# RWKV-5 attention followed by a smelu MLP on one core: blocks of 256 tokens in a written-out order, and one piece of smelu under a checked bound

## Chip, core and metric

The kernel runs on one core of a Trainium2 chip. The metric is the device time of one execution in microseconds (us). Five engines share the work: TensorE (PE, matrix products; PEld is its weight load), VectorE (DVE), ScalarE (ACT), GpSimd (POOL) and SyncE (SP), whose queue issues the DMAs here.

## What is computed

First an attention with a running state, for 4 batches, 8 heads, 768 tokens and 48 channels per head:

```
for t in range(S):
    cur = einsum('bhd,bhe->bhde', u[None] * kt, vt)
    y[:, :, t] = einsum('bhd,bhde->bhe', rt, state + cur)
    state = w[None, :, :, None] * state + einsum('bhd,bhe->bhde', kt, vt)
```

Its output is put together as x, 3072 tokens by 384 channels. Then an MLP with 2048 hidden channels:

```
h = x @ w_in
g = where(h >= 1, h, where(h <= -1, 0, (h + 1)**2 / 4))
out = g @ w_out
```

The function between the two products is smelu. For |h| <= 1 only its middle piece, (h+1)²/4, applies.

## The kernel before

**Attention.** The tokens of a batch are cut into 6 chunks of 128. A *unit* is one chunk c of one batch b; there are 24, ordered by chunk and then by batch. The generator `attention` (L151) makes one unit in five stretches that end at a `yield`.

1. *Preparation* (L156 to L168). K, R and V come in by three DMAs (`load`, L57, four units ahead). POOL writes K·Winv into `Kw` and R·Wpow into `Rw` (both padded to 64 channels a head, three buffers in turn), and K·u and then that times R into `KU`. ACT casts V to bf16, and DVE sums `KU` over each head into `diag`.
2. *Transposes* (L170 to L176). PE transposes the four head pairs of `Kw` and of `Rw` (8 instructions) into `tr`, and ACT copies it to `RK`.
3. *Scores* (L179 to L188). PE makes 8 products into two banks `AT_p`, and DVE multiplies each by the mask `umask` into `AT`.
4. *Output and state* (L190 to L228). PE adds up `st` (the state's increment) and `y`, POOL and DVE update the state `X` and its bf16 copy `Tbd`, POOL makes `VD` = V·diag, DVE adds x = VD + y.
5. *xT* (L230 to L233). PE transposes x in three pieces, and ACT copies them into the block's `xT`.

**MLP.** A block is one chunk of all four batches, so 512 tokens, and there are 6 blocks. `layer1(m, n)` (L240) makes 128 of the 2048 hidden channels: three matmuls with 512 columns into `h_p` (one PSUM bank), then smelu in three instructions: ACT clamps h (`cl`, L253), ACT squares it (`sq`, L254), DVE takes the larger of sq and h into `gT` (L255). `layer2(m, n)` (L259) makes four of the 16 matmuls with 384 columns that an output tile of 128 tokens takes; after the last, ACT copies `o_p` out (L273) and SP sends it to memory. The bf16 copies of the weights are made at first use, `w_in` on DVE (L245) and `w_out` on POOL (L265).

**Order.** The text (L291 to L303) first runs the four units of block 0, and then, for each block m and each n, layer1(m, n), layer2(m-1, n) and the next of the 20 attention stretches of block m+1. This is not the final order: the framework's scheduler orders each engine's queue by its own reckoning, so instructions of one engine may leave the order of the text. Within an engine the order is then fixed, and it waits on semaphores.

Of the kernel before, what the change touches and what calls it, by code (L numbers as in the profile page):

```python
# [16 lines left out]
def kernel(  # L17
# [11 lines left out]
    nc = tc.nc  # L29
# [10 lines left out]
    MT = B * C  # L40
# [14 lines left out]
    loaded = {}  # L55

    def load(i):  # L57
        b, c = units[i]
        t0 = c * C
        tiles = []  # L60
        for name, src in (("K", k), ("R", r), ("V", v)):
            t = io.tile([128, H, D], F32, name=name, tag=name)
            nc.sync.dma_start(out=t, in_=src[b, :, t0 : t0 + C, :].rearrange("h s d -> s h d"))
            tiles.append(t)
        loaded[i] = tiles
# [6 lines left out]
    u_bc = const.tile([128, H * D], F32, name="u_bc")  # L72
    nc.sync.dma_start(out=u_bc, in_=row_bcast(u))
    load(0)
# [9 lines left out]
    load(1)  # L84
# [3 lines left out]
    NQ = 4  # L88
    w_in_src = moe_w_in.rearrange("(ko ki) n -> ki ko n", ki=128)
    w_out_src = moe_w_out.rearrange("(no ni) d -> ni no d", ni=128)  # L90
    w_in_f, w_out_f = [], []
    for q in range(NQ):
        t = stage.tile([128, nKb, d_ff // NQ], F32, name=f"w_in_f{q}", tag="wf")
        nc.sync.dma_start(out=t, in_=w_in_src[:, :, q * (d_ff // NQ) : (q + 1) * (d_ff // NQ)])
        w_in_f.append(t)
        if q % 2 == 1:
            load(2 + q // 2)
    for q in range(NQ):
        t = stage.tile([128, nN // NQ, d_out], F32, name=f"w_out_f{q}", tag="wf")
        nc.sync.dma_start(out=t, in_=w_out_src[:, q * (nN // NQ) : (q + 1) * (nN // NQ), :])  # L100
        w_out_f.append(t)
# [9 lines left out]
    )  # L111
    i_int = const.tile([128, 1], mybir.dt.int32, name="i_int")
# [6 lines left out]
    nc.scalar.activation(lw, w_bc, AF.Ln)  # L119
    Wpow = const.tile([128, H, D], F32, name="Wpow")  # L120
# [3 lines left out]
    nc.scalar.activation(wc, wc, AF.Ln)  # L124
# [7 lines left out]
    NB = 3  # L132
    RWp, KWi = [], []
    for i in range(NB):
# [7 lines left out]
    for b in range(B):  # L142
# [3 lines left out]
        Tbd.append(t)  # L146


    xT = {}

    def attention(i):  # L151
        b, c = units[i]
        m = c
        if b == 0:
            xT[m] = gpool.tile([128, nKb, MT], BF16, name="xT", tag="xT")
        K, R, Vf = loaded.pop(i)  # L156
        if i + 4 < len(units):
            load(i + 4)
        Rw, Kw = RWp[i % NB], KWi[i % NB]
        nc.gpsimd.tensor_mul(Kw[:, :, 0:D], K, Winv)  # L160
        nc.gpsimd.tensor_mul(Rw[:, :, 0:D], R, Wpow)  # L161
# [3 lines left out]
        nc.gpsimd.tensor_mul(KU, K, u3)  # L165
        nc.gpsimd.tensor_mul(KU, KU, R)  # L166
        diag = work.tile([128, H], F32, name="diag", tag="diag")
        nc.vector.reduce_sum(diag, KU, axis=mybir.AxisListType.X)  # L168
        yield
        tr = ps_a.tile([128, 2 * NP, 128], BF16, name="tr", tag="a")  # L170
        for p in range(NP):
            nc.tensor.transpose(tr[:, NP + p, :], Kw[:, 2 * p : 2 * p + 2, :].rearrange("q h d -> q (h d)"), ident)  # L172
        for p in range(NP):
            nc.tensor.transpose(tr[:, p, :], Rw[:, 2 * p : 2 * p + 2, :].rearrange("q h d -> q (h d)"), ident)  # L174
        RK = work.tile([128, 2 * NP, 128], BF16, name="RK", tag="RK")
        nc.scalar.copy(RK, tr)  # L176
        RT, KT = RK[:, 0:NP, :], RK[:, NP : 2 * NP, :]
        yield
# [10 lines left out]
        yield  # L189
        if c < NCH - 1:  # L190
            st = ps_a.tile([128, NP, 2 * D], F32, name="st", tag="a")
            for p in range(NP):
                mm(
                    st[:, p, :], Kw[:, 2 * p : 2 * p + 2, :].rearrange("q h d -> q (h d)"),
                    V[:, 2 * p : 2 * p + 2, :].rearrange("q h d -> q (h d)"), start=True, stop=True,
                )
        y = ps_a.tile([128, H, D], F32, name="y", tag="a")
        first = True
        if c > 0:
            for p in range(NP):  # L200
                mm(  # L201
                    y[:, 2 * p : 2 * p + 2, :].rearrange("q h d -> q (h d)"), RT[:, p, :], Tbd[b][:, p, :],
                    start=first, stop=False, skip_group_check=True,
                )
                first = False
        for h in range(H):
# [4 lines left out]
            first = False  # L211
        if c < NCH - 1:
# [12 lines left out]
        VD = work.tile([128, H, D], F32, name="VD", tag="VD")  # L225
        nc.gpsimd.tensor_mul(VD, V, diag[:, :, None].to_broadcast([128, H, D]))  # L226
        x = work.tile([128, H * D], BF16, name="x", tag="x")
        nc.vector.tensor_add(x.rearrange("q (h d) -> q h d", h=H), VD, y)  # L228
        yield
# [3 lines left out]
        nc.scalar.copy(xT[m][:, :, b * C : (b + 1) * C], xp)  # L233
        yield


    gT = {}
    cast_in, cast_out = set(), set()

    def layer1(m, n):  # L240
        q = n // (nN // NQ)
        if q not in cast_in:
            cast_in.add(q)
            W = d_ff // NQ
            nc.vector.tensor_copy(w_in_sb[:, :, q * W : (q + 1) * W], w_in_f[q])  # L245
        if n == 0:
            gT[m] = gpool.tile([128, nN, MT], BF16, name="gT", tag="gT")
        h_p = ps_h.tile([128, MT], F32, name="h_p", tag="h")
        for kk in range(nKb):
            mm(h_p, w_in_sb[:, kk, n * 128 : (n + 1) * 128], xT[m][:, kk, :], start=(kk == 0), stop=(kk == nKb - 1))  # L250
        cl = ewp.tile([128, MT], F32, name="cl", tag="cl")
        sq = ewp.tile([128, MT], F32, name="sq", tag="sq")
        nc.scalar.activation(cl, h_p, IDENTITY_SAT240, scale=240.0)  # L253
        nc.scalar.activation(sq, cl, AF.Square, bias=0.5, scale=0.5 / 240.0)  # L254
        nc.vector.tensor_max(gT[m][:, n, :], sq, h_p)  # L255

    o_ps = {}

    def layer2(m, n):  # L259

        j, q = n // NQ, n % NQ
        if q not in cast_out:
            cast_out.add(q)
            W = nN // NQ
            nc.gpsimd.tensor_copy(w_out_sb[:, q * W : (q + 1) * W, :], w_out_f[q])  # L265
        if q == 0:
            o_ps[m, j] = ps_o.tile([128, d_out], F32, name="o_p", tag="o")
        o_p = o_ps[m, j]
        for f in range(q * (nN // NQ), (q + 1) * (nN // NQ)):
            mm(o_p, gT[m][:, f, j * C : (j + 1) * C], w_out_sb[:, f, :], start=(f == 0), stop=(f == nN - 1))  # L270
        if q == NQ - 1:
            o_sb = ewp.tile([128, d_out], F32, name="o_sb", tag="o_sb")
            nc.scalar.copy(o_sb, o_p)  # L273
            t0 = j * S + m * C
            nc.sync.dma_start(out=out[t0 : t0 + C, :], in_=o_sb)


    def attention_steps(m):
        for b in range(B):
            yield from attention(m * B + b)  # L280

    def drain(g, n):
        for _ in range(n):
            if next(g, "end") == "end":
# [49 lines left out]
```

## Time and profile before

| | us |
|---|---|
| median of 3 runs (lowest, highest) | 242.0 (240.9, 242.13) |
| the profiled execution | 240.13 |
| its span in the profile | 238.4 |
| busy: PE, ACT, POOL, DVE | 182.6, 164.3, 148.6, 137.2 |
| first matmul of the MLP starts at | 43.14 |

The profile is one execution. All rows below are on its time scale, which begins with the span. Busy times of PE overstate its work, since matmuls are pipelined and each one's row runs on into the next. The mean granted clock of TensorE was 0.97.

### The profile page before, as it was taken

How to read it: one execution, taken by the hardware profiler on the slowest of the kernel's cores; microseconds unless marked ns; L12 is line 12 of the kernel's file. 1: busy time of each engine (PE TensorE's matmuls, PEld its weight loads, DVE VectorE, ACT ScalarE, POOL GpSimd, SP SyncE). 2: the span in 40 equal slices, each digit the busy share in tenths (PEclk: the TensorE clock that was granted, in tenths of full speed). 3: DMA queues.
4: the chain of work that ended last, by engine and by line, in shares of the span. 5: the costliest groups of instructions: out<-in, count | busy, mean ns of one | idle time of the engine just before them, and what ended most of it. 6: DMA issues, size and time to landing. Idle time of an engine off the chain costs nothing.

```text
span 238.4 us, 4187 instructions
## 1 busy us (share of the span) xinstructions
PE 182.6 (77%) x1480; PEld 100.0 (42%) x1480; DVE 137.2 (58%) x245; ACT 164.3 (69%) x296; POOL 148.6 (62%) x197
## 2 busy tenths in 40 slices
PE   0033543796398296789797999899999999999994
PEld 0012322243255143445453545455555555445552
DVE  3008974167357426598656987688766666365400
ACT  3521312698469076969499897999979999699811
POOL 5297857979899998889999897955653000000000
PEclk9999999999859769999999999999999999999999
DMA  5999999945432048038775444400001001001121
GB/s 140 216 279 315 293 339 192 220 91 108 93 76 60 0 109 191 0 75 172 152 169 100 111 94 95 102 33 36 33 33 37 0 33 36 33 33 36 42 90 66
DMA packets 82772, 25.81 MB, mean 108 GB/s; under 512 B 75841, under 2 KB 81217, under 8 KB 82753
## 3 DMA queue, kind: packets, MB, share of 16 engines
q1 hardware_dynamic: 82752, 25.57, 43.9%
q8 instruction: 11, 0.18, 0.3%
q14 instruction: 9, 0.07, 0.1%
HBM read 20.84 MB, written 4.72 MB: 107 GB/s over the span
## 4 chain that ended last, share of the span: by engine, by line
PE 40%; POOL 22%; DVE 18%; issue 10%; ACT 7%; DMA 2%; SPq 0%; POOLq 0%; ACTq 0%; DVEq 0%
PE h_p L250 16%; PE o_p L270 16%; POOL KU L166 5%; POOL KU L165 4%; DVE gT L255 4%; POOL VD L226 3%; ACT sq L254 2%; ACT RK L176 2%; POOL KWi_158 L160 2%; POOL RWp_156 L161 2%; DVE x L228 2%; DMA K<-in_k_dram 2%; DVE diag L168 2%; ACT cl L253 2%; PE xp L232 2%
## 5 line engine op out<-in xcount | busy, mean ns | idle before, releaser
L250 PE MATMUL h_p<-xT,w_in_sb 128*128 128x512 bf16 x288 | 78.8, 391 | 9.7 <-DVE gT L255 9.1
L270 PE MATMUL o_p<-w_out_sb,gT 128*128 128x384 bf16 x384 | 80.8, 331 | 0.4 <-ACT o_sb L273 0.2
L255 DVE TENSOR_TENSOR gT<-sq,h_p 128x512 bf16<-128x512 f32 x96 | 64.0, 682 | 27.1 <-ACT sq L254 26.7
L253 ACT ACTIVATE cl<-h_p 128x512 f32<-128x512 f32 x96 | 56.2, 597 | 13.3 <-PE h_p L250 12.8
L254 ACT ACTIVATE sq<-cl 128x512 f32<-128x512 f32 x96 | 59.6, 635 | 1.6
L270 PEld LDWEIGHTS <-gT 128*128 128x128 bf16 x384 | 35.3, 98 | 25.2 <-issue 1.5
L168 DVE TENSOR_REDUCE diag<-KU 128x8 f32<-128x384 f32 x24 | 13.2, 551 | 50.8 <-POOL KU L166 40.1
L250 PEld LDWEIGHTS <-w_in_sb 128*128 128x128 bf16 x288 | 27.3, 100 | 34.4 <-issue 15.1
L233 ACT COPY xT<-xp 128x384 bf16<-128x384 bf16 x24 | 11.5, 477 | 26.2 <-PE xp L232 25.8
L176 ACT COPY RK<-tr 128x1024 bf16<-128x1024 bf16 x24 | 24.3, 1013 | 7.2 <-PE tr L174 7.2
L165 POOL TENSOR_TENSOR KU<-K,u_bc 128x384 f32<-128x384 f32 x24 | 24.0, 1001 | 2.2 <-DMA K<-in_k_dram 2.2
L226 POOL TENSOR_TENSOR VD<-V,diag 128x384 f32<-128x384 bf16 x24 | 19.9, 830 | 8.4 <-ACT V L163 6.6
L166 POOL TENSOR_TENSOR KU<-KU,R 128x384 f32<-128x384 f32 x24 | 24.0, 1002 | 0.4
L273 ACT COPY o_sb<-o_p 128x384 f32<-128x384 f32 x24 | 11.3, 474 | 14.2 <-PE o_p L270 14.1
L163 ACT CAST V<-V 128x384 bf16<-128x384 f32 x24 | 12.3, 513 | 5.7 <-DMA V<-in_v_dram 2.7
L228 DVE TENSOR_TENSOR x<-VD,y 128x384 bf16<-128x384 f32 x24 | 13.3, 553 | 1.0 <-PE y L207 0.4
L172 PE MATMUL tr<-ident,KWi_158 128*128 128x128 bf16 x32 | 3.8, 253 | 12.8 <-POOL KWi_158 L160 12.8
L160 POOL TENSOR_TENSOR KWi_158<-K,Winv 128x384 bf16<-128x384 f32 x8 | 8.0, 1001 | 8.7 <-ACT Winv L123 6.5
L232 PE MATMUL xp<-ident,x 128*128 128x128 bf16 x72 | 9.1, 243 | 4.8 <-DVE x L228 4.5
L183 PEld LDWEIGHTS <-RK 48*128 48x128 bf16 x192 | 5.9, 100 | 16.5 <-ACT RK L176 11.7
L201 PEld LDWEIGHTS <-RK 128*128 128x128 bf16 x80 | 5.5, 100 | 13.3 <-issue 10.8
L232 PEld LDWEIGHTS <-x 128*128 128x128 bf16 x72 | 5.1, 106 | 11.7 <-DVE x L228 10.9
(276 smaller groups left out, 248.0 us busy)
## 6 DMA issues: line engine op xcount, KB each, us to landing
K<-in_k_dram SPq DMA_DIRECT2D x24, 192.0 KB, 3.5
R<-in_r_dram SPq DMA_DIRECT2D x24, 192.0 KB, 3.5
V<-in_v_dram SPq DMA_DIRECT2D x24, 192.0 KB, 3.6
out_dram<-o_sb SPq DMA_DIRECT2D x24, 192.0 KB, 1.9
w_in_f_104<-in_moe_w_in_dram SPq DMA_DIRECT2D x1, 768.0 KB, 5.6
w_in_f_106<-in_moe_w_in_dram SPq DMA_DIRECT2D x1, 768.0 KB, 6.8
w_in_f_114<-in_moe_w_in_dram SPq DMA_DIRECT2D x1, 768.0 KB, 6.1
w_in_f_116<-in_moe_w_in_dram SPq DMA_DIRECT2D x1, 768.0 KB, 7.2
```

The lines of the kernel that those rows point to most:

```text
L165: nc.gpsimd.tensor_mul(KU, K, u3)
L166: nc.gpsimd.tensor_mul(KU, KU, R)
L168: nc.vector.reduce_sum(diag, KU, axis=mybir.AxisListType.X)
L176: nc.scalar.copy(RK, tr)
L226: nc.gpsimd.tensor_mul(VD, V, diag[:, :, None].to_broadcast([128, H, D]))
L228: nc.vector.tensor_add(x.rearrange("q (h d) -> q h d", h=H), VD, y)
L232: nc.tensor.transpose(xp[:, kk, :], x[:, kk * 128 : (kk + 1) * 128], ident)
L250: mm(h_p, w_in_sb[:, kk, n * 128 : (n + 1) * 128], xT[m][:, kk, :], start=(kk == 0), stop=(kk == nKb - 1))
L253: nc.scalar.activation(cl, h_p, IDENTITY_SAT240, scale=240.0)
L254: nc.scalar.activation(sq, cl, AF.Square, bias=0.5, scale=0.5 / 240.0)
L255: nc.vector.tensor_max(gT[m][:, n, :], sq, h_p)
L270: mm(o_p, gT[m][:, f, j * C : (j + 1) * C], w_out_sb[:, f, :], start=(f == 0), stop=(f == nN - 1))
```

## The change

The whole body from the pools down is rewritten in these respects.

- *Order.* Nearly everything is put in `tc.manual_schedule()`: each engine's queue follows the order of the text. The stretches of `attention` become five functions, `prep`, `s_tr`, `s_at`, `s_y` and `s_xp`, which the text calls in a written-out order.
- *Blocks.* A block is two units, 256 tokens; there are 12. `layer1(m, n)` makes two groups of 128 hidden channels, six matmuls with 256 columns into one PSUM bank. `layer2(m, n)` takes two hidden groups for both tiles of the block, four matmuls. All 12 `xT` are kept to the end.
- *smelu.* In the usual pass one ACT instruction, the square of (h+1)/2, goes from `h_p` to `gT`. Clamp, maximum and their buffers are gone there.
- *The bound.* |h| is at most |x||w| for the row x of a token and the column w of `w_in`. ACT sums x² for each token (`x2`, one more instruction a unit). POOL squares and adds up `w_in`, one quarter at a time, and PE and DVE finish the column sums (`w_norms`, 24 steps from step 48 of the main loop on). `bound_fails` compares the product of the two maxima with 0.95 and makes a flag. At the end all engines read the flag, and under `tc.If` a general pass (layer1 with clamp, square and maximum, and layer2) runs over all 12 blocks again.
- *Engines.* R·Wpow and K·u go from POOL to DVE. The casts of `w_in` are two pieces on DVE and one on ACT, those of `w_out` one on each. Half of the output copies go from ACT to DVE.
- *Buffers and loads.* Four instead of three `Rw`/`Kw`, six instead of five K, R, V, four PSUM banks for attention instead of three, two for `h_p` instead of three. At the start units 0 to 3 are loaded ahead of `w_in`, and the small loads for `wc` ahead of unit 0. The logarithm of `wc` goes ahead of the exponentials.

```
+    man = ExitStack()
+    man.enter_context(tc.manual_schedule())
...
+    def prep(i):
         K, R, Vf = loaded.pop(i)
+        Rw, Kw = RWp[i % NR], KWi[i % NR]
         nc.gpsimd.tensor_mul(Kw[:, :, 0:D], K, Winv)
-        nc.gpsimd.tensor_mul(Rw[:, :, 0:D], R, Wpow)
+        nc.vector.tensor_mul(Rw[:, :, 0:D], R, Wpow)
...
-        nc.gpsimd.tensor_mul(KU, K, u3)
+        nc.vector.tensor_mul(KU, K, u3)
         nc.gpsimd.tensor_mul(KU, KU, R)
...
+    def s_xp(i):
...
+        m, j = divmod(i, UB)
+        nc.scalar.copy(xT[m][:, :, j * C : (j + 1) * C], xp)
+        x2 = work.tile([128, H * D], BF16, name="x2", tag="x2")
+        nc.scalar.activation(x2, x, AF.Square, accum_out=xn[:, i : i + 1])
...
+    def layer1(m, n, general=False):
...
+        h_p = ps_h.tile([128, 2, MT], F32, name="h_p", tag="h")
+        for f in range(2):
+            for kk in range(nKb):
+                mm(
+                    h_p[:, f, :], w_in_sb[:, kk, (2 * n + f) * 128 : (2 * n + f + 1) * 128], xT[m][:, kk, :],
+                    start=(kk == 0), stop=(kk == nKb - 1),
+                )
+        g = gT[m][:, 2 * n : 2 * n + 2, :]
+        if not general:
+            nc.scalar.activation(g, h_p, AF.Square, bias=0.5, scale=0.5)
+        else:
+            cl = ewp.tile([128, 2, MT], F32, name="cl", tag="cl")
+            nc.vector.tensor_scalar(cl, h_p, -1.0, 1.0, ALU.max, ALU.min)
+            nc.scalar.activation(cl, cl, AF.Square, bias=0.5, scale=0.5)
+            nc.vector.tensor_max(g, cl, h_p)
+
+    def layer2(m, n):
...
+        for j in range(UB):
+            for f in (2 * n, 2 * n + 1):
+                mm(o_ps[m][j], gT[m][:, f, j * C : (j + 1) * C], w_out_sb[:, f, :], start=(f == 0), stop=(f == nN - 1))
...
+    def w_norms():
+        for q in range(NQ):
...
+            nc.gpsimd.tensor_mul(sq, wq, wq)
+            yield
+            nc.gpsimd.tensor_add(sq[:, 0, :], sq[:, 0, :], sq[:, 1, :])
+            yield
+            nc.gpsimd.tensor_add(sb, sq[:, 0, :], sq[:, 2, :])
+            yield
+            yield
+            yield
+            n_p = ps_a.tile([1, FQ], F32, name="n_p", tag="a")
+            mm(n_p, ones, sb, start=True, stop=True)
+            nc.vector.reduce_max(wn[:, q : q + 1], n_p, axis=mybir.AxisListType.X)
+            yield
...
+    prep(0)
+    prep(1)
+    s_tr(0)
+    s_tr(1)
+    s_at(0)
+    prep(2)
+    s_at(1)
+    s_y(0)
+    s_tr(2)
+    prep(3)
+    s_y(1)
+    s_at(2)
+    s_xp(0)
+    s_tr(3)
+    s_xp(1)
+    s_y(2)
+    s_at(3)
+    cast_in(0)
+    s_xp(2)
+    s_y(3)
+    layer1(0, 0)
+    s_xp(3)
+    layer1(0, 1)
+    cast_in(1)
+    layer1(1, 0)
...
+    for n in range(nP):
+        layer1(2, n)
+        if n % 2 == 1 and n < nP - 1:
+            cast_out(n // 2 + 1)
+        if n in (5, 7):
+            prep(6 + n // 7)
+        layer2(0, n)
+    for n in range(nP):
+        layer2(1, n)
+        stages[1 + n // 2](6 + n % 2)
...
+    G0 = 3 * nP
+    plan = {}
+    for m in range(4, NB):
+        for s in range(5):
+            for j in range(UB):
+                g = m * nP - 11 + 2 * s + j if m > 4 else G0 + s + j
+                plan.setdefault(max(g, G0), []).append((s, m * UB + j))
+    norms = w_norms()
+    for g in range(G0, NB * nP):
+        m, n = divmod(g, nP)
+        layer1(m, n)
+        for s, i in plan.get(g, ()):
+            stages[s](i)
+        layer2(m - 1, n)
+        if 6 * nP <= g:
+            next(norms, None)
+        if g == (NB - 1) * nP + 2:
+            flag = bound_fails()
+    for n in range(nP):
+        layer2(NB - 1, n)
...
+    man.close()
+    redo = nc.values_load(flag[0:1, 0:1], min_val=0, max_val=1, skip_runtime_bounds_check_because="a comparison's 0 or 1")
+    with tc.If(redo > 0):
+        for m in range(NB):
+            for n in range(nP):
+                layer1(m, n, general=True)
+            for n in range(nP):
+                layer2(m, n)
```

Between the two parts shown, the text lays the layer1 calls of blocks 0 and 1, the casts of `w_in` and the stages of units 4 and 5 in turn. `nP` is 8, `NB` 12 and `UB` 2; a step g of the main loop is one layer1 call, the stages planned for it, and one layer2 call.

245 lines of the change are left out of this document (132 added, 113 removed).

## Prediction

> **What bounds the kernel now.** I read the windows by stage first, then the waits, then the chain of work that ended last. In the windows the columns are the stretch and its length, busy time of PE, PEld, DVE, ACT and POOL, granted clock, DMA share and GB/s.
>
> ```profile
> 0.00:43.10 43.10, 13.04 (x124) 8.40 (x125) 20.28 (x37) 12.13 (x19) 29.30 (x51) 1.00 0.95 253
> 43.10:100.00 56.90, 41.91 (x319) 22.05 (x319) 30.36 (x56) 39.06 (x70) 52.30 (x63) 0.88 0.46 94
> 100.00:160.00 60.00, 53.25 (x482) 29.15 (x481) 44.68 (x83) 51.24 (x96) 53.73 (x69) 1.00 0.51 110
> 160.00:200.00 40.00, 39.63 (x351) 21.89 (x350) 27.79 (x48) 37.25 (x68) 13.28 (x17) 1.00 0.09 31
> 200.00:223.80 23.80, 23.77 (x144) 12.10 (x143) 12.77 (x21) 21.11 (x41) 0.00 (x0) 1.00 0.09 34
> 223.80:238.40 14.60, 11.01 (x68) 6.42 (x66) 1.37 (x2) 3.51 (x7) 0.00 (x0) 0.97 0.18 67
> ```
>
> There are three kernels here. Until 43.1 the MLP does not run at all. From 43.1 to 100 POOL is busy 52.3 of 56.9 while PE, at a mean clock of 0.88, issues 319 matmuls: POOL paces the stretch. From 160 on PE is busy 99%. The waits (us in total, times, longest) say the same: DVE waits for POOL's `KU`, not for its own work.
>
> ```profile
> DVE diag L168 <- POOL KU L166: 40.1, 11, 12.6
> ```
>
> So the floor is PE's own work. The chain's end gives its prices at full clock (start, duration, what):
>
> ```profile
> 214.03 0.65 PE h_p L250 x3
> 214.68 0.65 PE o_p L270 x4
> ...
> 223.76 11.06 PE o_p L270 x68
> ...
> 234.89 0.48 ACT o_sb L273
> ```
>
> Three matmuls of 512 columns take 0.65, so 0.216 each; 68 of 384 columns take 11.06, so 0.1626 each. Layer 1 is 288 × 0.216 = 62.2 and layer 2 is 384 × 0.1626 = 62.4. For the attention of one unit I take the stretch 160 to 200 where PE is full, with these rows for layer 1, layer 2 and the x transposes (busy and count come second):
>
> ```profile
> 160.00:200.00 40.00, 18.66 (x69) 1.00 0.09 31
> ...
> 160.00:200.00 40.00, 19.14 (x92) 1.00 0.09 31
> ...
> 160.00:200.00 40.00, 2.02 (x18) 1.00 0.09 31
> ```
>
> 69 × 0.216 + 92 × 0.1626 = 29.9 of the 39.63 is MLP, and 18 / 3 = 6 units share the other 9.8: 1.6 a unit. All of PE's work is then 62 + 62 + 24 × 1.6 = 163, against a span of 238.4. About 75 us can be won without a faster matmul, and they lie before 160.
>
> **The change, part by part.** The prices come from these groups (busy us, mean ns):
>
> ```profile
> L254 ACT ACTIVATE sq<-cl 128x512 f32<-128x512 f32 x96 | 59.6, 635 | 1.6
> L253 ACT ACTIVATE cl<-h_p 128x512 f32<-128x512 f32 x96 | 56.2, 597 | 13.3 <-PE h_p L250 12.8
> L176 ACT COPY RK<-tr 128x1024 bf16<-128x1024 bf16 x24 | 24.3, 1013 | 7.2 <-PE tr L174 7.2
> L163 ACT CAST V<-V 128x384 bf16<-128x384 f32 x24 | 12.3, 513 | 5.7 <-DMA V<-in_v_dram 2.7 <-PE y L207 2.5 <-issue 0.3
> L233 ACT COPY xT<-xp 128x384 bf16<-128x384 bf16 x24 | 11.5, 477 | 26.2 <-PE xp L232 25.8
> ```
>
> ```profile
> L255 DVE TENSOR_TENSOR gT<-sq,h_p 128x512 bf16<-128x512 f32 x96 | 64.0, 682 | 27.1 <-ACT sq L254 26.7
> L228 DVE TENSOR_TENSOR x<-VD,y 128x384 bf16<-128x384 f32 x24 | 13.3, 553 | 1.0 <-PE y L207 0.4
> L168 DVE TENSOR_REDUCE diag<-KU 128x8 f32<-128x384 f32 x24 | 13.2, 551 | 50.8 <-POOL KU L166 40.1 <-POOL VD L226 10.7
> L219 DVE TENSOR_TENSOR X_168<-X_168,st 48x192 f32<-48x192 f32 x8 | 2.8, 349 | 0.1
> ...
> L187 DVE TENSOR_TENSOR AT_519<-AT_p_509,umask 128x512 bf16<-128x512 f32 x1 | 0.7, 693 | 1.1 <-PE AT_p_510 L183 1.1
> ...
> L245 DVE CAST w_in_sb<-w_in_f_104 128x1536 bf16<-128x1536 f32 x1 | 1.7, 1746 | 0.0
> ```
>
> ```profile
> L166 POOL TENSOR_TENSOR KU<-KU,R 128x384 f32<-128x384 f32 x24 | 24.0, 1002 | 0.4
> L165 POOL TENSOR_TENSOR KU<-K,u_bc 128x384 f32<-128x384 f32 x24 | 24.0, 1001 | 2.2 <-DMA K<-in_k_dram 2.2
> L226 POOL TENSOR_TENSOR VD<-V,diag 128x384 f32<-128x384 bf16 x24 | 19.9, 830 | 8.4 <-ACT V L163 6.6 <-DVE diag L168 1.5
> ...
> L224 POOL TENSOR_TENSOR Tbd_173<-X_168,wc 48x192 bf16<-48x192 f32 x10 | 5.0, 505 | 2.8 <-DVE X_168 L219 1.9 <-DVE X_168 L221 0.6
> ...
> L265 POOL CAST w_out_sb<-w_out_f_130 128x1536 bf16<-128x1536 f32 x1 | 1.5, 1472 | 0.0
> ```
>
> *smelu.* One ACT square goes (59.6 or so), and DVE's 64.0 of maxima; the remaining pass, PSUM to bf16, is like `cl`, 0.60 for six matmuls. Neither engine bounds afterwards. ACT: 96 × 0.60 + 24 × (0.51 + 1.01 + 0.48, and 0.51 for the new x²) + about 12 of casts and output copies = 130. DVE: 24 × (two multiplies moved here at 0.55, diag 0.55, two `AT` at 0.69, x 0.55, two X at 0.35) = 24 × 4.3 = 103, and about 15 of casts, copies and maxima, 118. So smelu itself takes nothing off the path, since PE is the floor; it makes room. No row has DVE multiplying two SBUF tiles; x (one operand in PSUM) is the nearest, 0.55, against 1.00 on POOL.
>
> *POOL.* Two of its 1.00 multiplies a unit leave. Before, a unit takes 4 × 1.00 + 0.83 + two `Tbd` and one X multiply at 0.505 = 6.35, so four units of a block 25.4; after, 4.35. The w_out casts leave too.
>
> *Blocks of 256.* Price of a matmul by columns: (216 − 162.6) / 128 = 0.417 ns a column, so 256 columns take 0.109. Layer 1 becomes 576 × 0.109 = 62.9, dearer by 0.7. There are twice as many weight loads, 576 with this row's mean:
>
> ```profile
> L250 PEld LDWEIGHTS <-w_in_sb 128*128 128x128 bf16 x288 | 27.3, 100 | 34.4 <-issue 15.1
> ```
>
> I cost them at nothing: a load of 0.100 fits beside a matmul of 0.109, as it did beside one of 0.1626 in the row of 68. The cover is thin; without it 576 × 0.1 = 58 would come on top. I make that no case of its own, since every row so far has loads and matmuls overlapped. A block needs two units instead of four, which is what lets layer 1 start sooner.
>
> *The start.* ACT's queue now puts unit 0's V behind the tables; before, it stood in front (start, duration, idle before):
>
> ```profile
> 7.27 0.51 ACT L163 CAST V<-V 128x384 bf16<-128x384 f32 x1 [2.68 <-DMA V<-in_v_dram]
> 7.70 0.20 ACT L124 ACTIVATE wc<-wc 128x4 f32<-128x4 f32 x1
> ...
> 10.51 0.99 POOL L160 TENSOR_TENSOR KWi_158<-K,Winv 128x384 bf16<-128x384 f32 x1 [6.53 <-ACT Winv L123]
> ```
>
> The tables come 2.68 + 0.43 = 3.1 sooner, and `Kw` of unit 0 starts at 7.4. The logarithm of wc adds a wait for its two small DMAs, and all of ACT stands behind it. I cost it at nothing, as they are issued right behind the load of w, which ACT waits for anyway; without that cover it is 2.2 (their row stands below). From there DVE's order is longest: four units at 4.3, without the x and X of the last (1.25), with two of three casts of the first w_in quarter (2 × 1.75 / 3 = 1.2), 17.1; the rows overlap by some 0.08 each (two in a row here), about 30 of them, so 14.7. Waits: u comes after unit 0, 2; `KU` from POOL and back, 2.5. 7.4 + 14.7 + 4.5 = 26.6, say 26.5 for the first MLP matmul, against 43.1.
>
> ```profile
> 18.99 0.55 DVE L168 TENSOR_REDUCE diag<-KU 128x8 f32<-128x384 f32 x1 [3.09 <-POOL KU L166]
> 19.46 0.68 DVE L187 TENSOR_TENSOR AT_221<-AT_p_211,umask 128x512 bf16<-128x512 f32 x1
> ```
> SP's queue moves four units ahead of w_in: 2.8 MB and the first quarter's 0.8 at 253 GB/s take 14, so it lands before 18 and stays hidden; the w_out loads wait on SP for the w_in casts, and the loads of units 6 on wait behind them, some 15 us before they are needed.
>
> *From there on PE:* layers 62.9 + 62.4, 20 units × 1.6 = 32, the column sums and the rest of the prologue 1: 158.
>
> *Gaps in the fixed order, early.* In blocks 0 and 1 ACT has 16 × 0.60 + 3 × 0.58 + two units at 2.5 and the end of two more, 2: 18.3, less 0.08 of overlap each (V and wc above) for 30, 15.9; PE has 16 × 0.65 + 2 × 1.6 = 13.6. ACT is late by 2. In the loop with layer2(1) alone, stages follow each other by two steps, 2 × (0.65 + 0.4) = 2.1, where a copy of `RK` alone is 1.0 and needs transposes before and scores after: 3 in all. Sum 5; between 2 and 12.
>
> *Column sums.* On POOL, six steps take one multiply of 1536 columns and two adds of 512. By `Tbd` and `KU`, (1002 − 505) / 192 = 2.6 ns a column: 4.0 for the multiply; by `VD`, which has a bf16 operand, 4 × 0.83 = 3.3; by the cast with one operand 1.47. I take 3.5, near `VD`, and 1.33 an add: 6.2. The six steps also hold 1.5 units × 4.35 = 6.5, together 12.7. PE's time for them is 6 × 1.3 + 1.5 × 1.6 = 10.2. So POOL falls behind by 2.5 in each of four rounds, 10. `Kw` is wanted two steps after it is queued, 3.4, and takes 1.0, so the first 2.4 are covered: 8 on the path. Ends: 0 by the cast's price, 10 by 4.0.
>
> *Reading the flag and the jump.* Nothing in the trace does this. It removes nothing at the end, so it can't gain. The nearest row of something small fetched is a DMA of 0.8 KB:
>
> ```profile
> wc<-in_w_dram SPq DMA_DIRECT2D x2, 0.8 KB, 2.2
> ```
>
> One such time, 2.2; between 0 (engines that are done early) and 4.4 (one for the flag, one for far code). [...]
>
> *Tail:* from the last matmul's end, 234.82, to 238.4 is 3.6, and 240.13 − 238.4 = 1.7 lies outside the span.
>
> Sum: 26.5 + 158 + 5 + 8 + 2.2 + 3.6 + 1.7 = **205.0 us**. The profiled run is 0.8% under the median of 242.0; I take the sum as a median.
>
> **The rivals.**
>
> *POOL has room.* The squares go at the one-operand price and gaps stay at 2: 205 − 8 − 3 = 194. For it: both operands are the same bf16 tile. Against: no two-operand POOL row is under 2.1 ns a column.
>
> *DVE and POOL exclude each other.* If a DVE multiply with both operands in SBUF holds POOL off for its whole 0.55, then in the 24 steps with the column sums (6 units, 12 multiplies) 6.6 comes on top, and at the start, 8 multiplies, half on the path, 2.2: 205 + 9 = 214. For it: the only DVE multiplies of before have an operand in PSUM, and POOL's times stay at 1.001 to 1.003, so the trace excludes nothing. Against: nothing shows it. [...]
>
> *Hand-offs exposed on PE (slower).* With a fixed order PE can't pass a stage that isn't ready. In before's start, where PE has nothing else, a unit takes 5.75 by its x:
>
> ```profile
> 21.42 0.55 DVE x L228
> ...
> 27.17 0.56 DVE x L228
> ```
>
> That is 4.15 over its 1.6. If all 20 later units lay bare like that, 20 × 4.15 = 83 would stand in place of 5 + 8, 275 us. It decides from (240.1 − 192) / 20 = 2.4 a unit, 192 being the sum without gaps. Against: stages are two steps, 3.4 us, apart with MLP work between.
>
> *The change doesn't do what it says.* If the flag is set, the general pass follows: 125 of matmuls more, 330. From the reference's inputs the largest |x|² is 0.233 and the largest |w|² 1.286: product 0.30, far under 0.95.
>
> **How the numbers follow.** Chances: forecast 0.42, POOL has room 0.25, exclusion 0.25, hand-offs in part (220 to 239) 0.04, hand-offs to the end 0.02, general pass 0.01, within 0.5% of before 0.01. About 0.5% is what a measurement of this kernel tells from no change. The range takes the first three with their bounds: from 194 less the 2.2 of the jump, 192, to 214 with the upper ends of jump (2.2) and gaps (4), 220. Faster 0.96, same 0.01, slower 0.03.
>
> **What would show it.** First layer 1 matmul near 26.5; layer 1 rows near 0.65 for six; POOL without a gap from step 48 on, and PE's waits on `Kw` in the transposes there, about 8 us in total; PE over 95% busy in blocks 3 to 5; the last matmul at about 197.5. DVE multiplies well over 0.55, or POOL's 1.00 rows grown where DVE multiplies, would show exclusion. I am wrong if PE waits mainly on ACT or DVE in the main loop, or if PE's own rows are longer than at 512 columns.

## The result, and the profile after

The changed kernel takes 217.1 us (median of 4, 215.8 to 217.3) against 241.5 (median of 4, 240.7 to 242.1): a ratio of 0.898, 95% interval 0.893 to 0.903. That is faster, as forecast, and inside the range, but 12 us above the 205.0. The profiled execution took 217.3, with a span of 215.5.

The first view of after is the windows by stage. I cut them at the first layer 1 matmul, at the starts of blocks 3, 6 and 9 and at the last matmul's end. Columns: the stretch and its length, busy time of PE, PEld, DVE, ACT and POOL, granted clock, DMA share, GB/s.

```profile
0.00:27.80 27.80, 11.11 (x121) 8.11 (x122) 19.99 (x43) 13.54 (x25) 17.97 (x35) 1.00 0.90 215
27.80:67.70 39.90, 35.30 (x354) 26.55 (x353) 25.58 (x48) 28.14 (x55) 18.62 (x26) 1.00 0.88 217
67.70:111.60 43.90, 42.12 (x459) 31.53 (x459) 34.26 (x55) 28.85 (x60) 31.39 (x40) 1.00 0.59 127
111.60:165.80 54.20, 44.65 (x455) 31.02 (x453) 36.00 (x57) 29.92 (x60) 50.37 (x50) 0.98 0.30 67
165.80:209.60 43.80, 43.00 (x390) 31.00 (x389) 14.55 (x28) 22.50 (x45) 8.55 (x10) 0.98 0.11 38
209.60:215.50 5.90, 0.00 (x0) 0.00 (x0) 0.56 (x1) 0.18 (x1) 0.00 (x0) 0.95 0.23 76
```

The MLP starts at 27.8 in place of 43.1, and blocks 3 to 5 and 9 to 11 are PE's: 42 of 43.9 and 43 of 43.8 busy. Blocks 6 to 8, the 24 steps that carry the column sums, are not. They have about as many matmuls as blocks 3 to 5 (455 rows against 459) and take 10.3 longer, and there it is POOL that is busy, 50.4 of 54.2.

Next the waits of after (us in total, times, longest us):

```profile
POOL KU L180 <- DVE KU L179: 16.0, 9, 7.2
...
PE tr L187 <- POOL KWi_174 L174: 12.1, 3, 8.7
...
DVE diag L193 <- POOL KU L180: 10.2, 10, 2.0
...
PE tr L187 <- POOL KWi_178 L174: 3.4, 4, 1.7
...
PE tr L187 <- POOL KWi_182 L174: 2.7, 1, 2.7
...
PE tr L187 <- POOL KWi_186 L174: 2.4, 3, 1.5
```

DVE's wait for `KU` fell from 40.1 to 10.2. One long wait is new: POOL now waits 16.0 for DVE's K·u. PE's waits for `Kw` come to 20.6, of which 8.7 is the kernel's first and 8.5 lie in blocks 6 to 8.

Then the groups (busy us, mean ns), for the rows that the forecast priced:

```profile
L275 ACT ACTIVATE gT<-h_p 128x512 bf16<-128x512 f32 x96 | 57.4, 602 | 52.4 <-PE h_p L269 52.0
...
L180 POOL TENSOR_TENSOR KU<-KU,R 128x384 f32<-128x384 f32 x24 | 26.3, 1097 | 16.0 <-DVE KU L179 16.0
...
L179 DVE TENSOR_TENSOR KU<-K,u_bc 128x384 f32<-128x384 f32 x24 | 22.9, 953 | 1.2 <-DMA u_bc<-in_u_dram 1.2
...
L307 POOL TENSOR_TENSOR sq<-w_in_sb 128x1536 f32<-128x1536 bf16 x4 | 11.2, 2794 | 0.1
L175 DVE TENSOR_TENSOR RWp_184<-R,Wpow 128x384 bf16<-128x384 f32 x6 | 8.0, 1340 | 1.5 <-DMA R<-in_r_dram 1.5
...
L174 POOL TENSOR_TENSOR KWi_186<-K,Winv 128x384 bf16<-128x384 f32 x6 | 7.2, 1206 | 0.0
```

One smelu pass takes 0.602, as taken. The multiplies moved to DVE do not take 0.55: K·u averages 0.95, and the R·Wpow rows, which the view lists by buffer, go up to 1.34 in the mean. POOL's `KU` and `Kw` multiplies, which took 1.001 to 1.003 before, now average 1.10 to 1.21. The timeline of block 7 shows why (start, duration, idle before):

```profile
140.81 2.94 POOL L307 TENSOR_TENSOR sq<-w_in_sb 128x1536 f32<-128x1536 bf16 x1
...
141.07 3.10 DVE L175 TENSOR_TENSOR RWp_184<-R,Wpow 128x384 bf16<-128x384 f32 x1
...
143.71 1.30 POOL L174 TENSOR_TENSOR KWi_182<-K,Winv 128x384 bf16<-128x384 f32 x1
144.09 1.34 DVE L179 TENSOR_TENSOR KU<-K,u_bc 128x384 f32<-128x384 f32 x1
144.98 1.31 POOL L180 TENSOR_TENSOR KU<-KU,R 128x384 f32<-128x384 f32 x1
145.07 0.40 PE L187 MATMUL tr<-ident,KWi_182 128*128 128x128 bf16 x4 [2.70 <-POOL KWi_182 L174]
```

DVE's R·Wpow, which takes 0.55 where nothing holds it (its fastest row here, and its mean in the run on PSUM operands below), starts while POOL squares a quarter of w_in and ends only 0.42 after it. Then POOL's `Kw`, which stood behind the squares, is the one that is stretched, 1.30 in place of 1.00, and PE waits 2.70 for it. In these rows the two engines take turns: DVE's multiply, with two SBUF inputs, stands for 3.10 where 0.55 is the work, and POOL's for 1.30 where it is 1.00.

### The profile page after: what moved, and what is told of

Same layout as the page of the kernel before. It is cut to its first block, busy times and chain, and to the rows that moved or that the text cites. A ratio compares the mean times of both kernels' runs of the same rounds, so it can differ in the third digit from the quotient of the medians.

```text
span 215.5 us, 4626 instructions
## 1 busy us (share of the span) xinstructions
PE 176.2 (82%) x1773; PEld 128.2 (59%) x1773; DVE 130.9 (61%) x228; ACT 123.1 (57%) x243; POOL 126.9 (59%) x158
## 4 chain that ended last, share of the span: by engine, by line
PE 38%; POOL 31%; DVE 10%; issue 9%; ACT 5%; SPq 2%; DMA 2%; POOLq 0%; DVEq 0%; ACTq 0%
PE o_p L287 16%; PE h_p L269 14%; POOL KU L180 6%; POOL sq L307 5%; POOL sq L309 2%; DMA R<-in_r_dram 2%; POOL Tbd_202 L247 2%; POOL Tbd_199 L247 2%; POOL VD L195 2%; POOL sb L311 2%; POOL KWi_178 L174 2%; POOL Tbd_196 L247 2%; POOL KWi_174 L174 2%; ACT gT L275 1%; PE tr L187 1%
## 5 line engine op out<-in xcount | busy, mean ns | idle before, releaser
L275 ACT ACTIVATE gT<-h_p 128x512 bf16<-128x512 f32 x96 | 57.4, 602 | 52.4 <-PE h_p L269 52.0
L287 PE MATMUL o_p<-w_out_sb,gT 128*128 128x384 bf16 x384 | 77.8, 328 | 1.6 <-ACT o_sb L294 1.6
L269 PEld LDWEIGHTS <-w_in_sb 128*128 128x128 bf16 x576 | 56.5, 99 | 22.1 <-issue 4.6
L180 POOL TENSOR_TENSOR KU<-KU,R 128x384 f32<-128x384 f32 x24 | 26.3, 1097 | 16.0 <-DVE KU L179 16.0
L191 ACT COPY RK<-tr 128x1024 bf16<-128x1024 bf16 x24 | 24.4, 1021 | 14.9 <-PE tr L189 14.6
L179 DVE TENSOR_TENSOR KU<-K,u_bc 128x384 f32<-128x384 f32 x24 | 22.9, 953 | 1.2 <-DMA u_bc<-in_u_dram 1.2
L292 DVE COPY o_sb<-o_p 128x384 f32<-128x384 f32 x12 | 6.7, 557 | 21.5 <-PE o_p L287 19.7
L193 DVE TENSOR_REDUCE diag<-KU 128x8 f32<-128x384 f32 x24 | 13.0, 547 | 10.3 <-POOL KU L180 10.2
L307 POOL TENSOR_TENSOR sq<-w_in_sb 128x1536 f32<-128x1536 bf16 x4 | 11.2, 2794 | 0.1
L247 POOL TENSOR_TENSOR Tbd_199<-X_190,wc 48x192 bf16<-48x192 f32 x10 | 5.0, 504 | 9.3 <-DVE X_190 L242 8.9
L247 POOL TENSOR_TENSOR Tbd_193<-X_188,wc 48x192 bf16<-48x192 f32 x10 | 5.0, 503 | 8.1 <-DVE X_188 L242 6.7
L269 PE MATMUL h_p<-xT_204,w_in_sb 128*128 128x256 bf16 x48 | 7.6, 308 | 2.3 <-DVE w_in_sb L340 1.5
L175 DVE TENSOR_TENSOR RWp_184<-R,Wpow 128x384 bf16<-128x384 f32 x6 | 8.0, 1340 | 1.5 <-DMA R<-in_r_dram 1.5
```

The lines of the kernel that those rows point to most:

```text
L179: nc.vector.tensor_mul(KU, K, u3)
L247: nc.gpsimd.tensor_mul(Tbd[b][rows, :, s * D : (s + 1) * D], X[b][rows], wc3[rows])
L269: mm(h_p[:, f, :], w_in_sb[:, kk, (2 * n + f) * 128 : (2 * n + f + 1) * 128], xT[m][:, kk, :], start=(kk == 0), stop=(kk == nKb - 1),)
L275: nc.scalar.activation(g, h_p, AF.Square, bias=0.5, scale=0.5)
L287: mm(o_ps[m][j], gT[m][:, f, j * C : (j + 1) * C], w_out_sb[:, f, :], start=(f == 0), stop=(f == nN - 1))
L307: nc.gpsimd.tensor_mul(sq, wq, wq)
```

## The experiments

The theory: POOL's queue paces blocks 6 to 8, through the column sums and through DVE and POOL taking turns (exclusion). The rivals: the length of the hand-offs between engines paces them, whatever POOL has to do; or the turns cost nothing on the path. (Where an expectation uses letters, these are P, H and N.) Each ratio is to the kernel before, run on the same chip; its median there was 240.5 to 241.5, so a difference of 1 us between two runs need not come from the edit.

### The column sums: left out, and moved to ACT

```
-    def w_norms(): ...
+    nc.vector.memset(wn, 1.3)
+    def w_norms():
+        yield
```

> Leaves out the squares and column sums of w_in (their maximum is set to the constant 1.3); all else is the changed kernel, 217.07 us, whose blocks 6, 7 and 8 take 15.7 + 18.9 + 19.6 = 54.2 us in its profile against 14.3 each in blocks 4 and 5. [...] Rival H (the fixed order lays its hand-offs bare, whatever POOL has to do): only four matmuls go, the blocks stay at 18 and the time at 215 to 217.

206.0 us, ratio 0.853 (0.848 to 0.858): 11.1 less than the changed kernel, at the 206 that I had set down for the theory. By the starts of its smelu passes, blocks 6 to 8 fall from 54.2 to 42.5. The hand-offs are the same in this run, so it is POOL's work in its queue that paces those blocks, and not the hand-offs by themselves.

```
-            nc.gpsimd.tensor_mul(sq, wq, wq)
...
+            for kk in range(nKb):
+                nc.scalar.activation(sb[:, kk, :], wq[:, kk, :], AF.Square)
+                yield
...
+            for kk in range(nKb):
+                mm(n_p, ones, sb[:, kk, :], start=(kk == 0), stop=(kk == nKb - 1))
```

> The same column sums on other engines: twelve squares of 512 columns on ACT into bf16 (0.6 us each), added over the three row groups by PE's accumulation (12 matmuls of 512 columns instead of 4), POOL has no part. Theory P: blocks 6 to 8 fall to 14.9 each, the time to 208, the eight more matmuls (8 x 0.216 = 1.7) being what it stays above the run without sums. Rival H: 217. A third reading, that any engine with 6 us more in those blocks falls late, would give 215 or more, since ACT gets 7 us.

209.5, ratio 0.870 (0.866 to 0.874). This does the whole computation, and 7.6 us of the 11.1 are won all the same. The other 3.5 are about what its sums need of PE, twelve matmuls in place of four, busy for 3.2:

```profile
L312 PE MATMUL n_p<-sb,ones 128*1 128x512 bf16 x12 | 3.2, 378 | 0.0
```

### Shared reads: taken away, with a control

A DVE multiply can keep its place, its number of elements and its data type and yet read only one operand from SBUF, if the other lies in PSUM, as y does for x (0.553 in the kernel before). The first run also left K·u out, so that two things changed at once.

```
-    Wpow = const.tile([128, H, D], F32, name="Wpow")
+    Wpow = ps_t.tile([128, H, D], F32, name="Wpow")      # one PSUM bank, attention keeps three of four
...
-        nc.vector.tensor_mul(KU, K, u3)
-        nc.gpsimd.tensor_mul(KU, KU, R)
+        nc.gpsimd.tensor_mul(KU, K, R)
```

> No multiply on DVE has two operands in SBUF any more: the table Wpow lies in a PSUM bank (attention has three banks instead of four), and u is left out, so that KU is K times R in one POOL multiply, which POOL had before too. POOL keeps its work and the column sums. [...] Rival N (POOL simply has too much work, no exclusion): POOL's rows stay, the blocks stay over 52 and the time at 215 to 217.

208.6, ratio 0.867 (0.862 to 0.871). It fits exclusion, for which I had set down 207, but the instruction that was left out, and POOL's wait for it, could be the cause just as well. So two more runs: the bank alone (`bufs=4` to `bufs=3` for attention),

> The changed kernel with three PSUM banks for attention in place of four and nothing else: the control of the run without shared reads, which gave one bank away for its table. If a bank is worth nothing there, the time is that of the changed kernel, 217 us (216 to 218.5), and the 8.5 us of that run belong to the two multiplies. If attention needs the fourth bank, the time is longer by what PE then waits in the transposes, 219 to 222, and taking the shared reads away was worth more than 8.5.

217.9, ratio 0.909 (0.905 to 0.913): by the times the bank costs 0.8, about the spread of the runs. The trace agrees: the first layer 1 matmul starts 0.9 later (28.73 against 27.83). By the ratios (0.909 against 0.898) it would be more, some 2.6, but these are to the kernel before on different chips. And the same number of instructions, with PSUM operands in both:

```
+    Wpow in a PSUM bank, as above
-        nc.vector.tensor_mul(KU, K, u3)
+        nc.vector.tensor_mul(KU, K, Wpow)
```

> The changed kernel with as many instructions as it has, but both of VectorE's multiplies read one operand from PSUM: Wpow lies in a PSUM bank (three banks are left for attention), and K*u is made K*Wpow, so u is left out of the diagonal. Column sums stay. Against the control with three banks, 217.9 us, and the run that left K*u out altogether, 208.6. Exclusion between two engines that both read from SBUF: 208 to 211, VectorE's multiplies back at 0.55 us or so without 3 us cases, POOL's at 1.00. Rival, the 8.5 us came of the instruction that was left out, with POOL's wait for it, and not of exclusion: 216 to 218.

209.5, ratio 0.867 (0.861 to 0.873): 8.4 under its control by the times, 10 by the ratios. The groups of that run:

```profile
L181 POOL TENSOR_TENSOR KU<-KU,R 128x384 f32<-128x384 f32 x24 | 24.0, 1001 | 12.4 <-DVE KU L180 12.4
...
L175 POOL TENSOR_TENSOR KWi<-K,Winv 128x384 bf16<-128x384 f32 x24 | 24.1, 1003 | 5.6 <-DVE RWp L176 3.4 <-DMA K<-in_k_dram 1.7
...
L176 DVE TENSOR_TENSOR RWp<-R,Wpow 128x384 bf16<-128x384 f32 x24 | 13.2, 550 | 7.8 <-DMA R<-in_r_dram 5.0 <-ACT Wpow L138 2.5
...
L180 DVE TENSOR_TENSOR KU<-K,Wpow 128x384 f32<-128x384 f32 x24 | 13.1, 548 | 0.0
```

POOL still waits 12.4 for DVE's `KU`, so that wait is not what cost the time. What changed is that DVE's rows are at 0.55 and POOL's at 1.00. That shows exclusion to be the cause of some 8 us. Its windows by stage, cut at the same places of its own timeline, say where they lay:

```profile
0.00:26.50 26.50, 11.44 (x121) 8.33 (x122) 17.67 (x43) 13.59 (x25) 17.44 (x35) 1.00 0.91 217
26.50:65.90 39.40, 35.65 (x355) 26.82 (x353) 22.98 (x47) 27.48 (x53) 17.86 (x25) 1.00 0.94 228
65.90:108.90 43.00, 41.61 (x458) 31.92 (x458) 28.32 (x57) 29.18 (x62) 29.08 (x42) 1.00 0.59 128
108.90:157.80 48.90, 42.82 (x454) 31.00 (x452) 27.33 (x53) 28.62 (x59) 45.06 (x49) 1.00 0.32 74
```

Against after it saves 1.3 at the start, 0.5 and 0.9 in blocks 0 to 5, and 5.3 in blocks 6 to 8. Against its control, which lacks the bank too, the start saves 2.2 (26.55 against 28.73) and, by the starts of the smelu passes, the blocks save 1.4 before block 6 and 5.4 in 6 to 8.

### Neither, and both remedies

With neither column sums nor shared reads (K·u left out as well):

> No column sums (their maximum set to 1.3) and no multiply of VectorE that reads two SBUF tables (Wpow in a PSUM bank; u left out, so the diagonal is that of K*R, one multiply of POOL). Alone, the first gave 11.1 us less and the second 8.5. If the two costs were separate, 217.1 - 19.6 = 197.5. If the column sums are late only because VectorE's multiplies stand in POOL's queue and the reverse (one cost seen twice), what is shared is counted once: 202 to 205, of which PE's own work and the tail are 199.

201.5, ratio 0.839 (0.837 to 0.840). The two single gains, 11.1 and 8.5, do not add up to the 15.6 found here: some 4 us are the same microseconds. That is the second case, half a microsecond under its lower end. Blocks 6 to 8 of this run take 42.5, little more than PE is busy in them (the first row is blocks 0 to 2):

```profile
25.50:64.30 38.80, 35.31 (x358) 26.68 (x356) 21.29 (x43) 27.41 (x53) 17.79 (x25) 1.00 1.00 237
...
107.20:149.70 42.50, 41.35 (x452) 31.38 (x450) 23.06 (x45) 27.68 (x58) 25.28 (x38) 1.00 0.37 85
```

A version that computes everything, with the sums on ACT and the table of R·Wpow in PSUM:

> Both remedies together: squares of the columns on ScalarE and their sums on PE, POOL having no part in them, and the table of R*Wpow in a PSUM bank (K*u stays on VectorE). Sums on ScalarE alone gave 209.5. If exclusion costs the start and blocks 1 to 3 as well, the PSUM table takes off 2.2 us at the first layer 1 matmul and about 2 in blocks 1 to 3: 205 (202 to 207). If all that exclusion cost lay in blocks 6 to 8 beside the column sums, nothing is left for it to win: 209 to 210.

209.1, ratio 0.869 (0.865 to 0.873), 0.4 less than with the sums on ACT alone: the 205 was missed, and the time is that of the second case. But its condition does not hold, since exclusion also cost time outside blocks 6 to 8 (2.2 and 1.4 above). K·u still reads two SBUF tiles there and averages 0.82, so half of the exclusion was left. In the traces the table won 0.2 at the first layer 1 matmul (27.68 against 27.86) and 1.1 in blocks 3 to 5, nothing in 6 to 8, and 0.7 was lost in blocks 0 to 2, where the first matmuls probably ran slowly for longer (the third smelu pass starts 2.88 after the first, against 2.36 with the sums on ACT alone; see the last section). The bank that it takes costs 0.9 at the start in the control. It is the fastest of the kernels that do all of the work, by 8 us over the changed one, though not by more than the spread over the sums on ACT alone.

### The parts of the change, undone one at a time

The flag's reading and the conditional general pass left out (`redo = nc.values_load(...)` and all under `tc.If`):

> Leaves out the reading of the flag and the conditional general pass; the flag is still computed. If reading and jump are what lengthened the end from 3.6 us (before) to 5.8 us (after the last matmul), the time falls by 2.2 to 214.9. Rival: the end is longer because two output tiles are finished together and their DMAs go out one after the other; then the time stays within 0.5 us of 217.1.

215.1, ratio 0.894 (0.888 to 0.901): 2.0 less by the medians, though the interval overlaps that of the changed kernel (0.893 to 0.903). The traces are firmer. The last copy in the timeline of after and of this run (the spans end at 215.5 and 213.1):

```profile
209.68 0.56 DVE L292 COPY o_sb<-o_p 128x384 f32<-128x384 f32 x1 [5.21 <-PE o_p L287]
```

```profile
209.49 0.56 DVE L292 COPY o_sb<-o_p 128x384 f32<-128x384 f32 x1 [5.21 <-PE o_p L287]
```

From that copy's start to the end are 5.82 and 3.61, so the reading and the jump take 2.2 (5.82 − 3.61).

The two multiplies back on POOL:

```
-        nc.vector.tensor_mul(Rw[:, :, 0:D], R, Wpow)
+        nc.gpsimd.tensor_mul(Rw[:, :, 0:D], R, Wpow)
...
-        nc.vector.tensor_mul(KU, K, u3)
+        nc.gpsimd.tensor_mul(KU, K, u3)
```

> The changed kernel with R*Wpow and K*u back on POOL, where the kernel before had them; column sums stay. POOL's attention row list is then 6.35 us a unit. With exclusion (theory): blocks 6 to 8 hold 6 units and four rounds of sums at the 5.3 us that the profile after shows for a round, 6 x 6.35 + 4 x 5.3 = 59.3, against the 54.2 that these blocks take now with the multiplies on VectorE: 5 longer, 222 us (219 to 226), and VectorE's rows lose their 3 us cases. Rival, the move saves its full 2 us a unit on POOL (no exclusion): 6 units x 2.1 = 12.6 longer, 229 to 230. If the multiplies on VectorE cost as much as they save: 217.

238.3, ratio 0.987 (0.984 to 0.991), 21 us over the changed kernel and within 2% of the kernel before: above every case that I had set down. By the smelu passes, 2.7 of it lies at the start, 7.7 in blocks 3 to 5 and 9.5 in blocks 6 to 8. POOL's queue fits the direction (two units in block 6, timeline of this run):

```profile
138.48 1.00 POOL L174 TENSOR_TENSOR KWi<-K,Winv 128x384 bf16<-128x384 f32 x1
139.44 1.00 POOL L175 TENSOR_TENSOR RWp<-R,Wpow 128x384 bf16<-128x384 f32 x1
...
140.39 1.00 POOL L179 TENSOR_TENSOR KU<-K,u_bc 128x384 f32<-128x384 f32 x1
...
141.47 1.00 POOL L180 TENSOR_TENSOR KU<-KU,R 128x384 f32<-128x384 f32 x1
142.42 1.00 POOL L174 TENSOR_TENSOR KWi<-K,Winv 128x384 bf16<-128x384 f32 x1
...
143.47 0.40 PE L187 MATMUL tr<-ident,KWi 128*128 128x128 bf16 x4 [1.28 <-POOL KWi L174]
```

The second `Kw` stands behind four instructions of the first unit, and PE waits for it. That a full POOL is not needed for this, two blocks without column sums show: 4 and 5 take 16.4 and 17.3 (15.0 and 14.2 in after) with POOL idle for 3.5 and 5.0 of it:

```profile
90.00:106.40 16.40, 13.97 (x150) 10.34 (x150) 6.95 (x14) 9.29 (x21) 12.95 (x18) 1.00 0.44 97
106.40:123.70 17.30, 15.54 (x150) 10.97 (x150) 6.61 (x14) 9.29 (x20) 12.27 (x17) 0.90 0.42 92
```

So I had added up POOL's work over the blocks where its place in the queue was what counted, and in the second row a lower granted clock on PE (0.90) comes on top. How the 21 divides between the two was not tried. The run does say that the moved multiplies, with their exclusion, are worth far more than they cost.

Smelu in the three instructions of before (clamp and square on ACT, maximum on DVE), all else as changed:

> The changed kernel with smelu in the kernel before's three instructions (clamp and square on ScalarE, maximum on VectorE) in the usual pass; all else as changed. If smelu alone takes nothing off the path and only makes room: ScalarE has 123 + 60 = 183 us and VectorE 131 + 64 = 195 in a span of 215, and in blocks 6 to 8, where VectorE is busy 13.5 of 19 us, 8 x 0.68 fill it: 222 to 232 us. If the two engines bound once the maxima are back, the kernel falls back to the time before or past it: 238 to 250.

259.0, ratio 1.074 (1.065 to 1.083): slower than before, and past both expectations. An ordinary block (4 of this run) shows what I had missed:

```profile
109.50:126.60 17.10, 14.63 (x152) 10.39 (x152) 15.08 (x27) 14.03 (x28) 9.42 (x13) 1.00 0.41 89
```

DVE's work in a block is then 15.1, more than the 13.6 that PE needs by the prediction's count, and more than PE's rows show (14.6). I had set DVE's 195 against the span of 215, which holds a start and an end where DVE has little to do. In the stage itself DVE bounds before PE does, and the 2.0 that are left to 17.1 are probably the hand-offs from ACT to DVE and back to PE (this was not tried apart). Such blocks are not the largest part: some 20 of the 42 us lie in blocks 0 to 2 (27.6 to 89.7 by the first layer 1 matmul and the passes of smelu, against 27.8 to 68.6 in after), where PE's longest waits are for weights that DVE casts (5.4 for w_out, 4.9 for w_in). So smelu's short form does not only make room here: without it the rest of the change is a loss.

Without the written-out order (one line, the manual schedule, left out):

> The changed kernel without the order written out by hand: the same instructions, placed by the framework's scheduler. If the written order is what keeps PE fed (attention a few steps ahead of the layers, casts between), 222 to 240 us. If the order matters little beside PE's own work, 215 to 219.

230.1, ratio 0.953 (0.946 to 0.960). The order by hand is worth 13 us, and the time is in the first case.

### A version that failed

```
-        KU = work.tile(...); nc.vector.tensor_mul(KU, K, u3); nc.gpsimd.tensor_mul(KU, KU, R)    # in prep
+        nc.gpsimd.tensor_mul(KU, K, R); nc.vector.tensor_mul(KU, KU, u3)                          # in s_tr, before diag
...
-            nc.gpsimd.tensor_mul(sq, wq, wq)
+            for kk in range(nKb):
+                nc.scalar.activation(sq[:, kk, :], wq[:, kk, :], AF.Square); yield                # adds stay on POOL
...
-        if 6 * nP <= g:
+        if 4 * nP <= g:
```

> A version drawn from the runs so far: the squares of the columns on ScalarE, their adds on POOL, one instruction a step from step 32 on (POOL has 5 us of a 14 us block free there), one matmul a round on PE in place of three; and the diagonal's products taken out of the queue ahead of the second unit's Kw: K*R on POOL and then its product with u on VectorE, both in the step of the transposes. Sums on ScalarE with three matmuls a round gave 209.5, of which 8 matmuls of 0.39 are 3.1; with the waits on Kw in blocks 3 to 8 gone too, 2 or so: 204.5 (203 to 207). If VectorE's multiplies are held by POOL wherever they stand and PE waits for them: 208 to 210.

229.9, ratio 0.945 (0.935 to 0.955), 13 us worse than the changed kernel in place of 13 better. The exchange of the two products put a new wait on DVE, first in the waits and then in the timeline of this run:

```profile
DVE KU L191 <- POOL KU L190: 47.0, 21, 5.3
```

```profile
83.31 0.56 DVE L191 TENSOR_TENSOR KU<-KU,u_bc 128x384 f32<-128x384 f32 x1 [1.96 <-POOL KU L190]
...
84.37 2.48 DVE L209 TENSOR_TENSOR AT<-AT_p,umask 128x512 bf16<-128x512 f32 x4
...
85.11 0.33 PE L221 MATMUL y<-Tbd,RK 128*128 128x96 bf16 x4 [2.67 <-DVE AT L209]
```

Behind the waiting product stand the masks `AT`, and PE waits 2.67 for them. 4.4 of the 13 us lie ahead of the first layer 1 matmul (32.24 against 27.83), where no column sums run, so these come from the exchange alone; the rest was not divided. In the changed kernel it is POOL that waits for DVE, 16 us; where 12 of these stayed, in the run on PSUM operands, the time fell all the same. Whether spreading the sums over more blocks would help by itself is open, as both were changed at once.

## Why the prediction was right in sign and 12 us off

Step by step, with the run on PSUM operands (209.5) as the kernel without exclusion and the run with neither (201.5) as the one without sums too:

- **First layer 1 matmul.** Forecast 26.5. Without exclusion it starts at 26.55, in a kernel with one bank less, which costs 0.9 there; with exclusion at 27.83. So the working of the start was right to within 1 us.
- **PE's own work, 158 with about 1 for the sums and the rest.** The working by counts holds. A later block has 8 × 1.3 + 2 × 1.6 = 13.6 by it and takes 14.2 in the run with neither (42.5 for three), of which PE is busy 13.8. Layer 1 at 256 columns costs what I took, six matmuls in 0.65 (197.14 to 197.79 in the timeline of after), with twice the weight loads hidden (576 in place of 288, at 0.099 each).
- **Early gaps, 5 (2 to 12).** Too small. In the run with neither, the first layer 1 matmul stands at 25.74 and the last ends at 193.5: 167.8, against 156.8 by the counts above (96 × 1.3 + 20 × 1.6, the forecast's 158 without the sums and the prologue), so 11.0 of gaps: 6.2 in blocks 0 to 2 and some 0.5 in each later block. My working looked for single late engines in two places. The waits of PE in blocks 0 to 2 of that run come to 3.1: 0.8 of them are for casts of w_in on DVE, which the working left out, 0.6 for those on ACT, which it counted, and 0.8 for an output copy. A first stretch at about half rate (six matmuls' rows in 1.48 in place of 0.82, the last section) was not among my places either; how much of the other 3.1 it makes was not measured.
- **Column sums, 8 on the path, and 1 of PE's.** 7.2 without exclusion, from the first layer 1 matmul to the last matmul (6.4 of it in blocks 6 to 8). PE's waits on `Kw` in those blocks, forecast at about 8, are 8.5, but that is luck: 4.9 are left without exclusion. The square took 2.75 there, not the 3.5 taken, and the adds 1.27.
- **Reading the flag and the jump, 2.2.** 2.0 by the times, 2.2 by the traces.
- **Tail.** 5.9 from the last matmul to the end, 3.6 + 2.2 forecast.
- **Smelu "takes nothing off the path … it makes room".** Wrong for the new order, as the three-instruction run showed: 42 us hang on it.

The step that failed is the choice between the forecast and the rival in which *DVE and POOL exclude each other*. I gave it 0.25 against 0.42, because the trace of before excludes nothing. It happened, and its price was nearly right: 6.6 in the 24 steps and 2.2 at the start forecast; 5.4 there, 2.2 at the start and 1.4 between measured against the control; 8.4 in the times against 9. The second step that failed is a size, the early gaps: 5 forecast, 11.0 measured. With exclusion, 205 + 8.4 = 213.4; the remaining 3.7 are the gaps (+6.0) less the cheaper sums (−1.8), with +0.3 at the tail, and less the bank (−0.8) that the run on PSUM operands pays. That the rival's 214 lies so near 217 is in part luck: the gaps were taken 6.0 too short and the sums 1.8 too long.

The reason in the prediction was sound, that no row of before had a DVE multiply of two SBUF tiles beside POOL, but such silence is no evidence that the two do not collide: it was no ground for putting exclusion so far behind. Nor was exclusion a reason to leave the two multiplies on POOL: moved back, they cost 21 us.

"Hand-offs exposed" and "POOL has room" did not happen: PE is busy 42 of 43.9 in blocks 3 to 5, and the squares do delay blocks 6 to 8. The general pass, which would have given 330, did not run either.

## What to carry to other kernels

Before work goes from POOL to DVE, look at where the operands lie: here, with two in SBUF, DVE's multiplies took up to 1.34 in the mean and POOL's up to 1.21, and with one in PSUM 0.55 and 1.00 (a cast with one input took longer beside POOL too, see the last section). That was 8 of 217 us, although the move itself was still worth more than twice that. In an order written by hand, look at which instruction stands behind a wait, and not only at how busy an engine is: when the same product was placed so that DVE came to wait in place of POOL, at least 4.4 us were lost. And set an engine's work against the stage that it falls in, not against the span.

## What the runs showed of the hardware beside this

**The clock after a wait.** PE waits 2.37 for `Kw` at the end of block 8, and what follows runs slowly. Timeline and windows of after:

```profile
163.35 0.40 PE L187 MATMUL tr<-ident,KWi_174 128*128 128x128 bf16 x4 [2.37 <-POOL KWi_174 L174]
...
163.89 1.49 PE L287 MATMUL o_p<-w_out_sb,gT 128*128 128x384 bf16 x4
...
167.55 0.81 PE L287 MATMUL o_p<-w_out_sb,gT 128*128 128x384 bf16 x4
```

```profile
162.00:164.00 2.00, 0.65 (x9) 0.65 (x10) 1.71 (x2) 0.24 (x1) 2.00 (x3) 0.93 0.00 0
164.00:166.00 2.00, 2.00 (x7) 0.56 (x6) 1.08 (x3) 1.39 (x2) 2.00 (x3) 0.50 0.00 0
166.00:168.00 2.00, 2.00 (x17) 1.52 (x16) 1.07 (x3) 0.69 (x2) 2.00 (x3) 0.72 0.54 197
```

The granted clock falls to 0.50, and four matmuls take 1.49 in place of 0.81. By the column that cost PE 0.14 + 1.0 + 0.56 = 1.7 us after a wait of 2.4. Some 1.1 of it lies in blocks 6 to 8, for which the run on PSUM operands shows a clock of 1.00, and so in the 5.3 above. The wait of 2.70 that ends at 145 in block 7 had no such sequel: the clock is 1.00 in every window of 2 us from 142 to 150. In the profiled executions of the kernels with many waits the mean clock is 0.95 to 0.97 (multiplies on POOL, three-instruction smelu, scheduler's order, the failed version) against 0.99 to 1.00 in the others. So an exposed wait can cost more than its length, as the one of 2.37 did here.

**A slow start that the clock column does not show.** The first six layer 1 matmuls of after:

```profile
27.83 1.48 PE L269 MATMUL h_p<-xT_204,w_in_sb 128*128 128x256 bf16 x6
```

Six take 0.82 in the loop by the same measure. The next six take 1.40, with the granted clock at 1.00 in the first stage's window (27.80 to 67.70). The rows of single matmuls fall from 0.42 to 0.27 at 30.6. In the run without column sums, which has the same instructions up to there, it seems to last longer: the third smelu pass starts 2.88 after the first (29.33, 32.21), in after 2.51 (29.34, 31.85). There block 3 starts 0.8 later than in after (69.39 against 68.56 by its first smelu pass). So some 0.8 us between two profiled executions can be this. No run explains it.

**Casts on DVE.** 512 columns of w_in, f32 to bf16, in one instruction:

```profile
L340 DVE CAST w_in_sb<-w_in_f x8: 417/496/1054, 27.1 to 41.6; 128x512 bf16<-128x512 f32 x8
```

From 0.417 to 1.054 (minimum, median, maximum); before, 1536 columns in one took 1.746, or 0.58 for 512. The two long ones of these eight stand beside POOL instructions. Two pairs of casts, timeline of after:

```profile
27.11 0.75 DVE L340 CAST w_in_sb<-w_in_f 128x512 bf16<-128x512 f32 x2
...
33.49 1.39 DVE L340 CAST w_in_sb<-w_in_f 128x512 bf16<-128x512 f32 x2
...
33.72 0.88 POOL L195 TENSOR_TENSOR VD<-V,diag 128x384 f32<-128x384 bf16 x1 [0.73 <-DVE diag L193]
```

During the first pair POOL is idle (26.52 to 28.74), and it takes 0.75; the second stands beside POOL's `VD` and takes 1.39. So beside POOL a DVE cast with a single SBUF input took longer as well, here by 0.64 for the pair, and what was seen of the two multiplies is not the whole of exclusion in this kernel.
